# Linear attention with an ELU feature map: the program without an engine block

## The chip, the cores and the metric

The kernel runs on one core of a Trainium2 chip. A core has five engines, each with its own instruction stream: TensorE (PE, with its weight loads listed as PEld), VectorE (DVE), ScalarE (ACT), GpSimd (POOL) and SyncE (SP), which here only issues transfers. They meet through semaphores: an instruction can wait until a semaphore has a value, and can raise one when it is done. Sixteen DMA engines carry what the queues issue. The metric is the device time of one execution in microseconds (us), as the median of several runs; less is better. One execution more was recorded by the hardware profiler, and all rows quoted below come from it.

## The reference

For each of 32 heads with 2048 rows of 128 numbers, in bfloat16:

```python
phi_q = jnp.where(q > 0, q + 1, jnp.exp(q)) + 1e-6
phi_k = jnp.where(k > 0, k + 1, jnp.exp(k)) + 1e-6
kv  = einsum("bhsd,bhse->bhde", phi_k, v)      # 128 x 128 per head
z   = sum of phi_k over s                      # 128 per head
num = einsum("bhqd,bhde->bhqe", phi_q, kv)
den = einsum("bhqd,bhd->bhq", phi_q, z)[..., None] + 1e-6
return num / den
```

q, k, v and the output are 16.8 MB each, so 67 MB go through the DMA engines.

## The kernel before

A head is one step of a software pipeline. SP loads k, v and q of a head (512 KB each, line 389), ACT takes exp(k), DVE and POOL make phi(k) from it, PE accumulates phi(k)ᵀ·[1|v] into PSUM (line 428) and transposes q (line 452), ACT and DVE make phi(q) from the transposed q, PE multiplies it with the head's kv (lines 499 and 500), DVE divides (lines 522 to 540), and SP stores 512 KB (line 587). Six buffers hold inputs, ten hold outputs, so that several heads are in flight.

The order is written out by hand. Each operation is added to a `Plan` with an engine and a number, its key; `order` sorts the operations of each engine by key, and `emit` works out which semaphore values each operation has to wait for and writes the five streams. `run(e, eng)` in `emit` writes one stream: for each operation its waits (line 220), then the operation. The stream of PE has a loop in its middle: `run_loop` (line 197) emits the operations of six heads once and lets PE go over them five times, with registers that hold the semaphore values to wait for (lines 190 and 203). The other streams are written out in full. At the end of SP's stream stand waits for all output transfers (line 226), one for each of the eleven semaphores of the stores.

Where the streams stand in the program is what this change is about. The program has a main body. Building the program object (line 616) puts into it four small POOL memsets of constants and a barrier of all engines: each of the other four drains and raises one semaphore, POOL waits for four of these and raises a second semaphore by four, and each of the others waits for that. Then `nc.Block()` (line 320) opens a block; `@block.gpsimd`, `@block.sync` and so on open a body for each engine, which its engine enters by a branch out of the main body. When the block is closed, at the end of the `with` of line 284, each engine branches to a common end, where the same kind of barrier stands once more: drain, raise, and wait for the release by POOL. Instructions of that closing barrier carry line 284, those of the opening one line 616.

Of the kernel before, what the change touches and what calls it, by code (L numbers as in the profile page):

```python
# [20 lines left out]
class Plan:  # L21
# [10 lines left out]
    def add(self, eng, key, emit, reads=(), writes=(), dma=None, tag=None, kind=None, after=()):  # L32
        op = Op()
        op.eng, op.key, op.emit, op.dma, op.tag = eng, key, emit, dma, tag
        op.kind = kind or eng
        op.deps, op.needed, op.clock = list(after), False, None
        op.reads, op.writes = tuple(reads), tuple(writes)
        for r in op.reads:
            w = self.writer.get(r)
            if w is not None:  # L40
                op.deps.append(w)
            if r[0].startswith("bank"):
                op.deps += [x for x in self.readers.get(r, []) if x.eng != eng]
        for r in op.writes:
            w = self.writer.get(r)
            if w is not None and (w.eng != eng or w.dma):
                op.deps.append(w)
            op.deps += [x for x in self.readers.get(r, []) if x.eng != eng or x.dma]
        for r in op.reads:
            self.readers.setdefault(r, []).append(op)  # L50
        for r in op.writes:
            self.writer[r] = op
            self.readers[r] = []
        self.ops.append(op)
        return op
# [4 lines left out]
            out.setdefault(op.eng, []).append((op.key, i, op))  # L60
        return {e: [o for _, _, o in sorted(l, key=lambda x: x[:2])] for e, l in out.items()}

    def emit(self, nc, block, sems, dma_sem, loop):
        order = self.order()
        for op in self.ops:
            for d in op.deps:
# [65 lines left out]
        def sem_of(s):  # L132
            return dma_sem(s[1:]) if s[0] == "dma" else sems[s[0]]

        def emit_op(e, eng, op):
            last = op.emit(eng)
            if op.dma:
                last.then_inc(dma_sem(op.dma), 16)
            elif op.sem is not None:
                last.then_inc(sems[op.kind], 1)  # L140
# [25 lines left out]
        def set_up(e, eng, l0, n, turns):  # L166
            body = turns_of(order[e], l0, n, turns)
            most, step, entry, now = {}, {}, [], {}
            for _, row in body:
                for x, v, d in row:  # L170
                    assert step.setdefault(x, d) == d
                    most[x] = max(v, most.get(x, 0))
            for x, v in most.items():
                now[x] = v - step[x]
                if 0 < now[x] and order[e][l0 - 1].clock.get(x, 0) < now[x]:
                    entry.append((x, now[x]))
            asks, ends = [], {}
            for i, (_, row) in enumerate(body):
                ask = []
                for x, v, d in row:  # L180
                    if v > now[x]:
                        now[x] = v
                        ask.append((x, (d, v)))
                        ends[(d, v)] = i
                asks.append(ask)
            reg = {}
            for k, (d, v) in enumerate(ends):
                assert v > 0
                reg[(d, v)] = eng.alloc_register(f"turn_{k}")
                self.moves.append(lambda r=reg[(d, v)], v=v: eng.reg_mov(r, v))  # L190
            return body, asks, ends, entry, reg

        def run_loop(e, eng, turns, ready):
            body, asks, ends, entry, reg = ready
            for x, v in entry:
                eng.wait_ge(sem_of(x), v)
            with nc.Fori(0, turns, engines=OrderedEngineSet([eng.engine])):
                for i, (op, _) in enumerate(body):
                    for x, key in asks[i]:
                        eng.wait_ge(sem_of(x), reg[key])  # L200
                    for key, l in ends.items():
                        if l == i:
                            eng.reg_add(reg[key], reg[key], key[0])
                    emit_op(e, eng, op)

        def run(e, eng):
            ops, i = order[e], 0
            if e == "pe":
                l0, l1 = (next(x for x in range(len(ops)) if ops[x].tag == t) for t in loop[:2])
                turns = loop[2]  # L210
                assert (l1 - l0) % turns == 0
                ready = set_up(e, eng, l0, (l1 - l0) // turns, turns)
            while i < len(ops):
                if e == "pe" and i == l0:
                    run_loop(e, eng, turns, ready)
                    i = l1
                    continue
                op = ops[i]
                for s, v in waits[id(op)]:
                    eng.wait_ge(sem_of(s), v)  # L220
                emit_op(e, eng, op)
                i += 1
            if e == "sp":
                for name, n in counts.items():
                    if name[0] == "o":
                        eng.wait_ge(dma_sem(name), 16 * n)

        if "pool" in order:
            @block.gpsimd
            def _(g):  # L230
                run("pool", g)
        if "sp" in order:
            @block.sync
            def _(g):
                run("sp", g)
        if "act" in order:
            @block.scalar
            def _(g):
                run("act", g)
        if "pe" in order:  # L240
            @block.tensor
            def _(g):
                run("pe", g)
        if "dve" in order:
            @block.vector
            def _(g):
                run("dve", g)


def bass_standalone__linear_attn_elu__prompt_kernel(  # L250
# [18 lines left out]
    LAST = NH - 1  # L269
# [14 lines left out]
    with ExitStack() as es:  # L284
        def sb(name, shape, dt):
# [23 lines left out]
        sems = {e: es.enter_context(nc.semaphore(f"s_{e}")) for e in (  # L309
            "pool", "act", "pe", "dve", "emk", "rk", "phik", "kvs", "zs", "eq", "rq", "relu", "emq", "div0", "div2", "phix")}  # L310
# [6 lines left out]
            for i in range(c):  # L317
                dsems[(n, i)] = es.enter_context(nc.semaphore(f"s_{n}{i}"))

        block = es.enter_context(nc.Block())  # L320
        pl = Plan()

        def rows(x, h):
# [275 lines left out]
                store(0, 9, late, (0, 1, 2), bo)  # L599
                store(9, NT, late + 0.01, (3, 4, "t"), NBO)  # L600

        pl.emit(nc, block, sems, dma_sem, (("kv2", 1), ("num", LAST - 1), 5))


# [26 lines left out]
```

## Time and profile before

| | |
|---|---|
| time, median of 3 runs | 169.31 us (169.19 to 170.59) |
| the profiled execution's own time | 169.59 us |
| its span, from the first to the last instruction | 167.8 us |
| PE, DVE, ACT busy | 158.3, 154.2, 156.0 us |
| POOL busy | 100.8 us |
| DMA over the span | 67.25 MB, mean 401 GB/s |

The time of an execution is longer than the span, since it also holds what lies before the first and after the last instruction of the program. Busy time counts the work of the engines alone: waits, branches, drains, register moves and the issuing of transfers are not in it. Where such an instruction has a row, its engine has a q behind its name (SPq, PEldq): the row is that of the engine's sequencer. L284 is line 284 of the kernel. Starts in rows are in us from the start of the span, durations in ns where the row says so.

### The profile page before, as it was taken

The page shows a single profiled execution, that of the slowest core. Times are in us where ns is not written, and L with a number is a line of the kernel's source. Part 1 is how long each engine was busy: PE and PEld are TensorE (multiplying, and loading weights), DVE is VectorE, ACT ScalarE, POOL GpSimd, SP SyncE. Part 2 cuts the span into 40 slices and gives each one's busy share as a digit, 9 for nine tenths or more (in the row PEclk, how much of TensorE's full clock was granted, in tenths as well). Part 3 has the DMA queues.
Part 4 walks back from the last instruction along what each step waited for, and adds up shares of the span by engine and source line. Part 5 has one row for each costly group of instructions (what it writes and reads, how often), then busy time and mean ns, then how long its engine had stood idle before and what let it go on. Part 6 is the DMA issues. An engine that isn't in the chain of part 4 may idle for free.

```text
span 167.8 us, 6512 instructions
## 1 busy us (share of the span) xinstructions
PE 158.3 (94%) x3143; PEld 151.3 (90%) x2449; DVE 154.2 (92%) x302; ACT 156.0 (93%) x143; POOL 100.8 (60%) x69
## 2 busy tenths in 40 slices
PE   7579999999999999999999999999999999999960
PEld 0259999999999999999999999999999999999950
DVE  0479999999999999999999999999999999999991
ACT  3969999999999999999999999999999999998790
POOL 2405677666666776666677766666777666666300
PEclk9999999999999999999999999999999999999996
DMA  5999999999999999999999999999999999999975
GB/s 192 367 419 421 413 410 416 413 421 408 414 417 416 419 418 417 421 419 416 414 419 421 415 417 422 416 417 420 418 419 419 420 415 417 421 418 415 410 242 221
DMA packets 19885, 67.25 MB, mean 401 GB/s; under 512 B 2082, under 2 KB 2210, under 8 KB 19874
## 3 DMA queue, kind: packets, MB, share of 16 engines
q1 hardware_dynamic: 19872, 67.12, 99.4%
q8 instruction: 5, 0.08, 0.2%
q14 instruction: 6, 0.05, 0.1%
q10 hardware_dynamic: 2, 0.00, 0.0%
HBM read 50.33 MB, written 16.78 MB: 400 GB/s over the span
## 4 chain that ended last, share of the span: by engine, by line
PE 85%; DVE 5%; DMA 4%; ACT 1%; SPq 1%; issue 0%; DVEq 0%
PE kvz_ps L428 35%; PE o_ps L499 17%; PE o_ps L500 16%; PE xT_ps L452 15%; DMA k_sb<-in_k_dram 4%; DVE o_sb L540 3%; PE kvz_ps L346 1%; ACT ek_sb L396 1%; SPq L389 1%; DVE rden_sb L528 1%; DVE rq_sb L472 0%; DVE emq_sb L484 0%; DVE den_sb L522 0%; DVE emk_sb L402 0%; DVE o_sb L533 0%
## 5 line engine op out<-in xcount | busy, mean ns | idle before, releaser
L407 POOL TENSOR_TENSOR rk_sb<-rk_sb,emk_sb 128x640 bf16<-128x640 bf16 x30 | 41.9, 1397 | 45.8 <-DVE emq_sb L484 44.5
L428 PE MATMUL kvz_ps<-v_sb,rk_sb 128*128 128x128 bf16 (+1 forms) x512 | 68.0, 218 | 0.9 <-DVE rk_sb L407 0.9
L540 DVE TENSOR_TENSOR o_sb<-o_ps,rden_sb 128x768 bf16<-128x768 f32 (+2 forms) x62 | 67.8, 1134 | 0.0
L399 POOL TENSOR_SCALAR rk_sb<-k_sb 128x2048 bf16<-128x2048 bf16 x31 | 58.7, 1895 | 9.5 <-DMA k_sb<-in_k_dram 9.5
L396 ACT ACTIVATE ek_sb<-k_sb 128x2048 bf16<-128x2048 bf16 x32 | 61.5, 1921 | 3.0 <-DMA k_sb<-in_k_dram 2.9
L463 ACT ACTIVATE eq_sb<-xT_ps 128x2048 bf16<-128x2048 bf16 (+1 forms) x33 | 60.1, 1825 | 3.3 <-PE xT_ps L452 2.2
L500 PE MATMUL o_ps<-kvs_sb,rq_sb 128*128 128x129 bf16 (+1 forms) x536 | 61.1, 217 | 0.0
L499 PE MATMUL o_ps<-kvs_sb,emq_sb 128*128 128x129 bf16 (+1 forms) x536 | 61.1, 217 | 0.0
L346 PE MATMUL kvz_ps<-ones_sb,rk_sb 128*128 128x1 bf16 x428 | 58.5, 165 | 0.0
L428 PE MATMUL kvz_ps<-v_sb,emk_sb 128*128 128x128 bf16 (+1 forms) x334 | 53.9, 218 | 0.8 <-DVE emk_sb L402 0.7
L499 PEld LDWEIGHTS o_ps<-kvs_sb,emq_sb 128*128 128x128 bf16 x536 | 50.6, 98 | 0.0
L500 PEld LDWEIGHTS o_ps<-kvs_sb,rq_sb 128*128 128x128 bf16 x536 | 50.1, 97 | 0.0
L428 PEld LDWEIGHTS kvz_ps<-v_sb,rk_sb 128*128 128x128 bf16 x512 | 46.4, 96 | 3.0 <-DVE rk_sb L407 1.8
L346 PE MATMUL kvz_ps<-ones_sb,emk_sb 128*128 128x1 bf16 x253 | 41.5, 165 | 0.0
L452 PE MATMUL xT_ps<-ident,q_sb 128*128 128x128 bf16 x512 | 33.8, 219 | 1.2 <-DMA q_sb<-in_q_dram 0.9
L452 PEld LDWEIGHTS xT_ps<-ident,q_sb 128*128 128x128 bf16 x512 | 29.9, 98 | 5.4 <-DMA q_sb<-in_q_dram 4.4
L428 PEld LDWEIGHTS kvz_ps<-v_sb,emk_sb 128*128 128x128 bf16 x334 | 32.1, 96 | 1.1 <-DVE emk_sb L402 0.8
L470 ACT ACTIVATE rq_sb<-xT_ps 128x1024 bf16<-128x1024 bf16 x30 | 30.5, 1018 | 0.0
L402 DVE TENSOR_SCALAR emk_sb<-ek_sb 128x2048 bf16<-128x2048 bf16 x32 | 21.9, 683 | 5.2 <-ACT ek_sb L396 5.2
L472 DVE TENSOR_SCALAR rq_sb<-xT_ps 128x1024 bf16<-128x1024 bf16 x34 | 23.3, 690 | 0.6 <-ACT eq_sb L463 0.6
L484 DVE TENSOR_SCALAR emq_sb<-eq_sb 128x2048 bf16<-128x2048 bf16 x32 | 22.0, 688 | 0.0
L533 DVE TENSOR_TENSOR o_sb<-o_ps,rden_sb 128x128 bf16<-128x128 f32 x31 | 9.0, 291 | 1.1
(29 smaller groups left out, 52.2 us busy)
## 6 DMA issues: line engine op xcount, KB each, us to landing
k_sb<-in_k_dram SPq DMA_DIRECT2D x32, 512.0 KB, 14.4
q_sb<-in_q_dram SPq DMA_DIRECT2D x32, 512.0 KB, 14.1
v_sb<-in_v_dram SPq DMA_DIRECT2D x32, 512.0 KB, 14.4
out_dram<-o_sb SPq DMA_DIRECT2D x30, 512.0 KB, 15.1
out_dram<-o_sb SPq DMA_DIRECT2D x1, 288.0 KB, 3.2
out_dram<-o_sb SPq DMA_DIRECT2D x1, 256.0 KB
out_dram<-o_sb SPq DMA_DIRECT2D x1, 224.0 KB, 3.1
out_dram<-o_sb SPq DMA_DIRECT2D x1, 204.0 KB
```

What stands on the lines that cost most here:

```text
L346: return pe.add_instruction(mybir.InstMatmult(start_tensor_calc=start, stop_tensor_calc=stop, ldweights=False, bass_skip_group_check=True, ...
L396: lambda a, bi=bi, b2=b2: a.activation(ek_sb[:, b2, :], k_sb[:, bi, :], ACT.Exp),
L399: lambda e, bi=bi, b3=b3: e.tensor_scalar(rk_sb[:, b3, :], k_sb[:, bi, :], BIG, 0.0, op0=ALU.min, op1=ALU.max),
L407: pl.add(eng, key, lambda e: e.tensor_tensor(out=rk_sb[:, b3, c], in0=rk_sb[:, b3, c], in1=emk_sb[:, b3, c], op=ALU.add), reads=[("emk", b ...
L428: last = pe.matmul(kvz_ps[:, 1 - l:NC + r], lhsT=w, rhs=v_sb[:, bi, c - l:c + D + r], start=first, stop=fin, skip_group_check=True)
L452: last = pe.transpose(xT_ps[:, j * P:(j + 1) * P], q_sb[:, bi, j * P:(j + 1) * P], ident[:])
L463: halves[part] = pl.add("act", key, lambda a: a.activation(eq_sb[:, b2, c], xT_ps[:, c], ACT.Exp), reads=both[part:part + 1] or both, writ ...
L470: f = lambda a: a.activation(rq_sb[:, b3, c], xT_ps[:, c], ACT.Relu)
L472: f = lambda d: d.tensor_scalar(rq_sb[:, b3, c], xT_ps[:, c], 0.0, None, op0=ALU.max)
L499: pe.matmul(o_ap, lhsT=emq_sb[:, b3, t * P:(t + 1) * P], rhs=kvs_sb[:, b3, c0:c1], start=True, stop=False)
L500: return pe.matmul(o_ap, lhsT=rq_sb[:, b3, t * P:(t + 1) * P], rhs=kvs_sb[:, b3, c0:c1], start=False, stop=True)
L540: pl.add("dve", key, lambda d: d.tensor_tensor(out=o_sb[:, bo, 3 * g0:3 * g1, :].rearrange("p (a b) d -> p a b d", b=3), in0=_ap(full, bas ...
```

## The change

The block is gone. `emit` is no longer handed a block, and writes the five streams one after the other into the main body, right behind the opening barrier; PE comes last, since its loop opens new parts of the program, and whatever is written behind them would stand there too. The operations, their order on each engine, their waits and PE's loop are as before. Behind the last instruction of an engine nothing follows: no branch to a common end, no drain, and no barrier.

```diff
-    def emit(self, nc, block, sems, dma_sem, loop):
+    def emit(self, nc, sems, dma_sem, loop):
...
-        if "pool" in order:
-            @block.gpsimd
-            def _(g):
-                run("pool", g)
-        if "sp" in order:
-            @block.sync
-            def _(g):
-                run("sp", g)
-        if "act" in order:
-            @block.scalar
-            def _(g):
-                run("act", g)
-        if "pe" in order:
-            @block.tensor
-            def _(g):
-                run("pe", g)
-        if "dve" in order:
-            @block.vector
-            def _(g):
-                run("dve", g)
+        for e, eng in (("pool", nc.gpsimd), ("sp", nc.sync), ("act", nc.scalar), ("dve", nc.vector), ("pe", nc.tensor)):
+            run(e, eng)
...
-        block = es.enter_context(nc.Block())
...
-        pl.emit(nc, block, sems, dma_sem, (("kv2", 1), ("num", LAST - 1), 5))
+        pl.emit(nc, sems, dma_sem, (("kv2", 1), ("num", LAST - 1), 5))
```

## The prediction

> **What bounds the kernel now.** The time of three stages has to be told apart: the start, the long middle, and the end. The first view is the table by windows, with cuts at the first transfer (0.8 us), at the full pipeline (13 us), at the last heads (156 us), at the last compute (164.2 us) and at the last wait for a transfer (167.4 us). Columns are the window, its length, the busy time of PE, PEld, DVE, ACT and POOL with the number of instructions, PE's clock, the DMA share and GB/s.
>
> ```profile
> 0.00:0.80 0.80, 0.00 (x0) 0.00 (x0) 0.00 (x0) 0.00 (x0) 0.27 (x5) 1.00 0.00 0
> 0.80:13.00 12.20, 9.24 (x91) 3.86 (x59) 5.91 (x13) 8.43 (x7) 2.77 (x5) 1.00 0.92 350
> 13.00:156.00 143.00, 142.88 (x2938) 141.66 (x2296) 140.35 (x271) 140.28 (x119) 96.95 (x60) 1.00 1.03 417
> 156.00:164.20 8.20, 6.19 (x123) 5.82 (x97) 7.89 (x21) 7.28 (x18) 0.81 (x1) 1.00 0.87 324
> 164.20:167.40 3.20, 0.00 (x0) 0.00 (x0) 0.00 (x0) 0.00 (x0) 0.00 (x0) 0.56 0.54 209
> 167.40:167.80 0.40, 0.00 (x0) 0.00 (x0) 0.00 (x0) 0.00 (x0) 0.00 (x0) 0.50 0.00 0
> ```
>
> In the middle, PE is busy for 142.88 of 143.00 us, and the DMA engines are full too. The change touches no operation there, so those 143 us move only if PE is held up by its own instruction stream; that is the third rival below. What the change does touch lies in the first window, in which the opening barrier ends and the streams are entered, and in the last one, 0.40 us in which no engine computes and no transfer runs. Behind the span there is more: the execution took 169.59 us, the span 167.8, so 1.79 us lie before the first or after the last instruction, and no row shows how they are shared out.
>
> The second view is the chain of work that ended last, with the page's head.
>
> ```profile
> span 167.8 us, 6512 instructions
> ...
> PE 85%; DVE 5%; DMA 4%; ACT 1%; SPq 1%; issue 0%; DVEq 0%
> ```
>
> The 85% for PE is the middle. This chain is followed back from the last computing instruction, so the end barrier is not in it and has to be read from the rows of its line, and from the waits of SP's queue.
>
> **The end, row by row.** The instructions of the closing barrier carry line 284. Columns: engine, instruction, count, duration in ns (min/median/max), first and last start in us.
>
> ```profile
> L284 POOLq EVENT_SEMAPHORE  x2: 17/17/17, 167.6 to 167.7; - x2
> L284 POOLq DRAIN  x1: 1502/1502/1502, 155.4 to 155.4; - x1
> L284 PEldq DRAIN  x1: 723/723/723, 161.7 to 161.7; - x1
> L284 ACTq DRAIN  x1: 911/911/911, 163.1 to 163.1; - x1
> L284 DVEq DRAIN  x1: 1091/1091/1091, 163.1 to 163.1; - x1
> L284 SPq COMPARE_BRANCH  x1: 38/38/38, 167.4 to 167.4; - x1
> L284 SPq DRAIN  x1: 7/7/7, 167.6 to 167.6; - x1
> L284 SPq EVENT_SEMAPHORE  x1: 17/17/17, 167.7 to 167.7; - x1
> L284 ACTq EVENT_SEMAPHORE  x1: 17/17/17, 167.7 to 167.7; - x1
> L284 DVEq EVENT_SEMAPHORE  x1: 21/21/21, 167.7 to 167.7; - x1
> L284 PEldq EVENT_SEMAPHORE  x1: 51/51/51, 167.7 to 167.7; - x1
> ```
>
> The waits for the stores, and what SP waited for there:
>
> ```profile
> L226 SPq EVENT_SEMAPHORE  x5: 28/28/28, 164.6 to 167.3; - x5
> ```
>
> ```profile
> SPq L226 <- DMA out_dram<-o_sb: 2.5, 1, 2.5
> ...
> SPq L284 <- PEq L284: 0.2, 1, 0.2
> ```
>
> The reader is to see who comes last. Four engines drained long before: POOL's drain starts at 155.4, PE's at 161.7, ACT's and DVE's at 163.1 us, and each has ended by 164.2 (163.1 plus 1.09). SP waits 2.5 us for the stores and passes the last wait of line 226 at 167.3. Then comes the hand-over: SP's branch at 167.4, its drain at 167.6, POOL's two semaphore instructions at 167.6 and 167.7, and the four releases at 167.7, of which PE's is the longest with 51 ns and closes the span at 167.8. Nothing covers this: the window from 167.4 on is empty.
>
> **What the change removes there.** Line 226 has only five semaphore rows. A branch waits for nothing of its own kind, and it stands where the wait for the eleventh store semaphore has to be; I take it that this last wait rides on the branch. Without a branch it needs an instruction of its own, priced by its neighbours at 28 ns against the branch's 38. So what remains is a wait at 167.4, and the span ends at its end. Removed are the 0.40 us of the last window less the branch's own 0.04: **0.36 us**. The starts are rounded to 0.1 us, so by the rows alone the term lies between 0.26 and 0.46. What is late next is the same store: its landing sets the time of SP's last wait, and nothing in the change moves a store.
>
> The four drains that go too cost nothing, as they lie beside the stores' 3.20 us; the cover would be gone only if an engine drained after 167.4. DVE's drain of 1091 ns starts ahead of its last division's end and waits for it, not the other way about, so the last store starts no earlier without it.
>
> **The start.** The opening barrier (line 616) stays, and SP's first load comes straight behind it.
>
> ```profile
> L616 POOLq EVENT_SEMAPHORE  x2: 17/17/17, 0.5 to 0.6; - x2
> ...
> L616 SPq EVENT_SEMAPHORE  x1: 17/17/17, 0.7 to 0.7; - x1
> L616 ACTq EVENT_SEMAPHORE  x1: 17/17/17, 0.7 to 0.7; - x1
> L616 DVEq EVENT_SEMAPHORE  x1: 21/21/21, 0.7 to 0.7; - x1
> L616 PEldq EVENT_SEMAPHORE  x1: 51/51/51, 0.7 to 0.7; - x1
> ```
>
> ```profile
> 0.73 0.39 SPq L389 DMA_DIRECT2D k_sb<-in_k_dram  x1
> 1.18 0.42 SPq L389 DMA_DIRECT2D q_sb<-in_q_dram  x1
> ```
>
> Had the branches into the block been executed, there would be a branch row for each engine here; neither line 616 nor line 284 has one at the start. The release is at 0.7 and the first load at 0.73, while the second load comes 0.06 us after the first ended (1.12 to 1.18), so the gap ahead of the first is no longer than the plain distance of two of SP's instructions. I price the entry at 0. The ends are 0 and, if SP did lose something between 0.65 and 0.73, a gain of 0.08. The opening barrier also gives the closing one a second price: from POOL's first semaphore instruction (0.5) to the last release (0.7 and 51 ns) it took 0.2 to 0.3 us, to which SP's branch and drain come at the end. That agrees with 0.36.
>
> **The sum.** Against the profiled execution: 169.59 − 0.36 − 0 = 169.23 us. That execution lies 0.28 above the median of the three runs, so the time to expect is 169.31 − 0.36 = **168.95 us**, 0.2% less. The three runs of before spread over 1.4 us, so about 1% is what a measurement of this kernel can tell from no change, and the forecast is "within 1%".
>
> **The rivals.**
>
> *More goes than the span shows.* After the change four engines reach their end between 157 and 164 us, and only SP at 167.4. If each engine has closing work behind its last instruction, that of four engines moves beside the stores, and out of the 1.79 us outside the span a part goes as well. For it: that stretch exists and today all engines enter it together. Against: SP has the same work and is still last; only engines slower at it than SP can give a gain. Half of it, 0.9 us, gives 169.31 − 0.36 − 0.9 = 168.05; all of it, 167.16.
>
> *The barrier is paid under another name.* Something behind the program still has to know that all engines are done. If that costs SP's signal and a release as now, the span is shorter by 0.36 and the stretch behind it longer by as much: 169.31. For it: 1.79 us outside the span are more than nothing. Against: whatever stands there stood there before too, behind the kernel's own barrier, so the two were paid one after the other. The Trainium skill, Runtime: NRT & Kernel Launch, section The ~15µs preamble/postamble breakdown, says that the runtime closes each launch with a barrier of its own over all engines, at about 1.5 us. By that rule the wait for all engines stays whatever the kernel does, and whether this rival or the forecast holds depends on whether the four early engines can stand in that barrier already; no row of this trace shows it.
>
> *PE's loop has to fetch its code again (slower).* PE's stream is moved from the block's body into the main body; its loop head may come to lie elsewhere in what the engine holds of its code. The rows of code fetches, from the view of DMA queues for 0 to 45 us and then for 45 to 168 us, and of the loop's closing branch:
>
> ```profile
> q8 instruction: 5, 0.08, 0.7%
> q14 instruction: 1, 0.01, 0.0%
> ```
>
> ```profile
> q14 instruction: 5, 0.04, 0.1%
> ```
>
> ```profile
> L197 PEldq COMPARE_BRANCH  x5: 76/213/231, 41.9 to 156.9; - x5
> ```
>
> Queue q8 fetched five pieces of 16 KB by 45 us and none after, so I take it for PE's, and the loop was held whole: four times PE jumped back (the fifth branch, the one of 76 ns, falls through), and the middle's 0.12 us of idle time show no stall. One fetch takes 0.7% of 16 engines for 45 us, 5.0 us, over five pieces: 1.0 us. If the moved loop no longer fitted, each of four returns would wait for at least one piece, and PE has no slack in the middle: 4 × 1.0 − 0.36 = 3.6 us more, 172.95. It decides as soon as the jump's target is no longer held; a single stall at the loop's entry would give 168.95 + 1.0 = 169.95. Against it: if the entry branches left no instruction behind, PE's stream ahead of the loop is as long as before. The same page of the Trainium skill, section Instruction fetch mechanics, says that a taken branch whose target isn't in a window of two pages forces a fetch before execution goes on. By that rule the four jumps, over some 28.75 us of work each, would have paid already; the trace disagrees, with 0 pieces of q8 behind 45 us.
>
> **How the numbers follow.** The forecast gets 0.60 (168.6 to 169.2), the larger gain 0.20 (167.2 to 168.6), no gain 0.12 (169.2 to 169.6), and the loop 0.08, of which 0.05 for the returns and 0.03 for one stall at the entry. Faster by over 1% means below 167.6, the far part of the larger gain: 0.05. Slower by over 1%, above 171.0: the returns, 0.05. The rest is 0.90. The range runs from 168.1, which takes in half of the larger gain, to 169.6, the end of no gain: 0.60 + 0.12 + 0.10 = 0.82.
>
> **What would show it.** Right: no row of line 284, the span at about 167.4, its last instruction a wait of line 226 (now six such rows) at 167.4 and 28 ns; the first load still at 0.73; five pieces on q8, all by 45 us; the middle at PE's 142.9 us of 143. The first rival shows as a distance between time and span well below 1.79, the second as one of 2.15. The third shows as pieces on q8 after 45 us and idle PE behind the branches, at 41.9 us and every 28.75 us from there ((156.9 − 41.9) / 4). I am wrong if any of the middle's period changes, or if engines that end early do something that reaches the stores: then the last wait's 167.4 moves.

## The result and the profile after

The changed kernel takes 168.38 us (168.18 to 168.99, 8 runs) against 169.39 us (169.13 to 170.59, 8 runs) before: ratio 0.9935, 95% interval 0.9908 to 0.9962. Run again on another occasion, it took 168.54 against 169.32 us, ratio 0.9956 (0.9940 to 0.9973). So it is faster by 0.8 to 1.0 us, about half a per cent and clear of the noise, where 0.36 was forecast.

Each run gives its time and its span, so the gain can be parted in two. Before, in 29 runs taken beside the rerun, the median span was 167.5 us and the time outside the span, that is time less span, 1.81 us on average (1.75 to 1.87). After, over the 14 runs of both occasions, the median span is 167.15 and the time outside 1.31 us (1.26 to 1.37). The span fell by 0.35, the time outside by 0.50, together 0.85 us. The time outside differs by about 0.1 us from run to run, so its fall is clear in every single run; the fall of the span has to be read from medians, since spans of one kernel differ by more than that.

The windows of the profiled execution after (168.30 us, span 167.0), from the full pipeline on, cut at the last heads, the last compute and the last wait; the columns are as before the change:

```profile
13.00:156.00 143.00, 142.89 (x2931) 141.45 (x2294) 140.30 (x270) 139.69 (x119) 96.93 (x60) 1.00 1.03 417
156.00:163.90 7.90, 5.93 (x118) 5.58 (x92) 7.64 (x20) 7.26 (x18) 0.56 (x1) 1.00 0.87 335
163.90:166.97 3.07, 0.00 (x0) 0.00 (x0) 0.00 (x1) 0.00 (x0) 0.00 (x0) 0.65 0.56 215
166.97:167.00 0.03, 0.00 (x0) 0.00 (x0) 0.00 (x0) 0.00 (x0) 0.00 (x0) 0.50 0.00 0
```

The middle is as full as before, PE busy 142.89 of 143.00 us. The last window, 0.40 us before, is 0.03 us long: one wait. The rows of a closing barrier are gone, and the waits for the stores have six rows (eleven semaphores, so some rows hold more than one), the last of them at the span's end:

```profile
L226 SPq EVENT_SEMAPHORE  x6: 17/28/1880, 164.3 to 167.0; - x6
```

At the start nothing has moved. The opening barrier (now line 597) releases SP at 0.7 us as before, and SP's first load after the change is this one:

```profile
0.73 0.39 SPq L370 DMA_DIRECT2D k_sb<-in_k_dram  x1
...
```

The two profiled spans differ by 0.8 us, more than the medians do. The last window explains 0.37 of it. The other 0.43 lies ahead of the last window: the last store was issued 0.3 us earlier (163.9 against 164.2), and it landed 3.0 us after its issue, against 3.1. PE was ahead by 0.3 us already at its loop's first branch (41.6 against 41.9 us), and this came in at the start, where ACT waits for k of the second head. The rows of the exp(k) that starts then, from the timelines of before, of the changed kernel, and of the changed kernel run again:

```profile
9.35 1.91 ACT L396 ACTIVATE ek_sb<-k_sb 128x2048 bf16<-128x2048 bf16 x1 [1.23 <-DMA k_sb<-in_k_dram]
```

```profile
8.84 1.91 ACT L377 ACTIVATE ek_sb<-k_sb 128x2048 bf16<-128x2048 bf16 x1 [0.82 <-DMA k_sb<-in_k_dram]
```

```profile
8.10 1.91 ACT L377 ACTIVATE ek_sb<-k_sb 128x2048 bf16<-128x2048 bf16 x1
```

The same program started it at 8.84 once and at 8.10 another time, and the kernel before with a second barrier at its end (below) at 8.34. But an earlier start did not bring an earlier end. The changed kernel run again issued its last store at 163.2, 0.7 us earlier than the first time, and its span is 167.2, longer than 167.0, because this store took longer to land. Its rows from the first and the second profile of the changed kernel (KB, us from issue to landing):

```profile
out_dram<-o_sb SPq DMA_DIRECT2D x1, 224.0 KB, 3.0
```

```profile
out_dram<-o_sb SPq DMA_DIRECT2D x1, 224.0 KB, 3.9
```

So when the first loads and the last store land differs from one execution to the next, and a single pair of profiles can't price a change of 0.4 us.

### The profile page after: what moved, and what is told of

The parts are those of the page before. It is cut to its first block, busy times and chain, and to the rows that moved or that the text cites. A ratio compares the mean times of both kernels' runs of the same rounds, so it can differ in the third digit from the quotient of the medians.

```text
span 167.0 us, 6501 instructions
## 1 busy us (share of the span) xinstructions
PE 158.5 (95%) x3143; PEld 151.4 (91%) x2449; DVE 154.3 (92%) x302; ACT 155.9 (93%) x143; POOL 100.8 (60%) x69
## 4 chain that ended last, share of the span: by engine, by line
PE 86%; DVE 6%; DMA 4%; ACT 1%; SPq 1%; issue 0%; DVEq 0%
PE kvz_ps L409 36%; PE o_ps L480 17%; PE o_ps L481 17%; PE xT_ps L433 16%; DMA k_sb<-in_k_dram 4%; DVE o_sb L521 3%; PE kvz_ps L327 1%; ACT ek_sb L377 1%; SPq L370 1%; DVE rden_sb L509 1%; DVE o_sb L514 0%; DVE rq_sb L453 0%; DVE emq_sb L465 0%; DVE den_sb L503 0%; DVE emk_sb L383 0%
## 5 line engine op out<-in xcount | busy, mean ns | idle before, releaser
L388 POOL TENSOR_TENSOR rk_sb<-rk_sb,emk_sb 128x640 bf16<-128x640 bf16 x30 | 41.9, 1396 | 46.1 <-DVE emq_sb L465 44.8
```

What stands on the lines that cost most here:

```text
L388: pl.add(eng, key, lambda e: e.tensor_tensor(out=rk_sb[:, b3, c], in0=rk_sb[:, b3, c], in1=emk_sb[:, b3, c], op=ALU.add), reads=[("emk", b ...
```

## The experiments

Two theories stood against each other. **The end:** all of the gain comes from four engines ending early; the closing barrier held them, and each has something to do behind its last instruction that counts into the time. **The place of the code:** the part outside the span comes from the streams standing in the main body. A third, that a barrier as such costs 1 us, goes by the same runs.

**The barrier put back, without the block.** Added to the changed kernel:

```diff
         pl.emit(nc, sems, dma_sem, (("kv2", 1), ("num", LAST - 1), 5))
+        nc.all_engine_barrier()
```

> The changed kernel with one barrier of all engines behind its last wait, and still no block. Theory 'the end': the whole gain comes from four engines ending early, 0.36 to 0.43 us inside the span and 0.5 us behind it. Then the time is that of the kernel before within 0.2 us: span up by 0.35 to 0.4, outside back at 1.8 us. Rival 'the place of the code': the gain outside the span comes from the streams standing in the main body without branches into a block. Then outside stays at 1.3 us, and the time is 0.5 us below the kernel before.

Measured: 169.19 us against 169.32 before, ratio 0.9994 (0.9976 to 1.0012), and 1.80 us outside the span in its 11 runs. The place of the code falls: the streams stand in the main body, and the whole 0.50 outside the span is back. The rows of its barrier (line 584), and of its waits for the stores:

```profile
L584 POOLq EVENT_SEMAPHORE  x2: 17/17/17, 167.6 to 167.7; - x2
L584 POOLq DRAIN  x1: 1502/1502/1502, 155.3 to 155.3; - x1
...
L584 SPq DRAIN  x1: 7/7/7, 167.6 to 167.6; - x1
...
```

```profile
L226 SPq EVENT_SEMAPHORE  x6: 17/28/1991, 164.5 to 167.5; - x6
```

The expectation missed one size. The median span, 167.4, is 0.15 above the changed kernel's on the same chip (167.25), not 0.35 to 0.4; against all 14 runs of the changed kernel (167.15) it is 0.25. Medians of so few runs can't decide between these, since the spans of this version alone lie between 167.2 and 168.4. The rows are sharper: from the last wait at 167.5 to the span's end at 167.8 lie about 0.3 us, and SP's drain comes right behind the wait. In the kernel before, SP's branch stood between, at 167.4 with the drain only at 167.6. So by these rows, whose starts are rounded to 0.1 us, some 0.1 of the forecast's 0.36 was the way out of the block, and the rest the barrier. The times can't tell that 0.1 from nothing (0.9976 to 1.0012).

**A second barrier in the kernel before.** Added behind the closed block:

```diff
         pl.emit(nc, block, sems, dma_sem, (("kv2", 1), ("num", LAST - 1), 5))
+    nc.all_engine_barrier()
```

> The kernel before with a second barrier of all engines behind the block's. Theory 'the end': the span grows by the barrier's own hand-over alone, 0.2 to 0.3 us (from POOL's first semaphore instruction to the last release), and the time outside stays at 1.8 us, since all engines ended late already: 0.2 to 0.3 us slower than before (ratio 1.0015). Rival 'each barrier costs 1 us': the time grows by as much as the change took off, 1.0 us (ratio 1.006).

Measured: 169.59 against 169.32, ratio 1.0020 (1.0008 to 1.0032); median span 167.8 against 167.5; 1.80 us outside. A barrier in which nobody is early costs 0.27 us (by the interval, 0.14 to 0.54), its hand-over. Its rows (line 603), behind those of the block's:

```profile
L603 POOLq EVENT_SEMAPHORE  x2: 17/17/17, 167.6 to 167.7; - x2
L603 POOLq DRAIN  x1: 46/46/46, 167.5 to 167.5; - x1
L603 SPq DRAIN  x1: 7/7/7, 167.5 to 167.5; - x1
...
L603 PEldq EVENT_SEMAPHORE  x1: 51/51/51, 167.8 to 167.8; - x1
```

From the drains at 167.5 to the last release at 167.8: 0.3 us, in line with the difference of the times. That a barrier costs 1 us each time falls with it.

**All engines late, without a barrier.** In the changed kernel each engine, not SP alone, waits for the stores at its end:

```diff
-            if e == "sp":
+            if True:
                 for name, n in counts.items():
                     if name[0] == "o":
                         eng.wait_ge(dma_sem(name), 16 * n)
```

> The changed kernel in which all five engines, not SP alone, wait for the eleven store semaphores at their end; no barrier. Theory 'the end': the span is that of the changed kernel within 0.1 us (no hand-over), but all engines now end late, so the time outside goes back to 1.8 us: 0.5 us slower than the changed kernel. Rival 'the barrier itself': only drains and the hand-over cost, so the time outside stays at 1.3 us and the time is that of the changed kernel.

Beside it, on the same chip, ran the changed kernel again:

> The changed kernel once more, beside the experiments. Both theories: 1.0 us less than the kernel before (ratio 0.994), span near 167.0 us, and 1.3 us outside the span (1.8 in the kernel before).

Measured: 168.91 us (12 runs) with all engines waiting, 168.54 (6 runs) with SP alone. The median span is 167.05 against 167.25, so no cost shows inside; outside it is 1.83 against 1.31 us. The rows of line 226 show all five leaving the last wait together:

```profile
L226 POOLq EVENT_SEMAPHORE  x6: 17/42/1962, 159.5 to 166.9; - x6
L226 PEldq EVENT_SEMAPHORE  x6: 51/51/1962, 160.7 to 166.9; - x6
L226 ACTq EVENT_SEMAPHORE  x6: 17/38/1962, 162.1 to 166.9; - x6
L226 DVEq EVENT_SEMAPHORE  x6: 21/50/1964, 162.1 to 166.9; - x6
L226 SPq EVENT_SEMAPHORE  x6: 17/28/1962, 163.6 to 166.9; - x6
```

So the 0.50 us is neither drain nor hand-over: it is the price of engines other than SP ending late, with a barrier or without one. The span and the time outside are two terms, and this run moves the second.

**Which engine.** The eleven waits were moved from SP to one other engine each, by the same line (`if e == "pe":` and so on), and then given to all but POOL (`if e != "pool":`).

> The changed kernel with the eleven last waits on PE in place of SP, so that PE alone ends late. Theory 'one slow engine': each engine has closing work of its own length behind its last instruction, and the 1.8 us of the kernels in which all end late is that of the slowest, SP's being 1.3. If PE is the slowest: 1.8 us outside, time 0.5 us above the changed kernel; if not, 1.3 or less. Rival 'a chain': the closing is a hand-over from engine to engine, and what it costs depends on where in the chain the late engine stands; then the five engines give five values in steps, between some 0.9 and 1.8.

> The changed kernel with the eleven last waits on ACT in place of SP. Theory 'one slow engine': 1.3 us outside the span or less, unless ACT is the slow one (1.8). Rival 'a chain': a value of its own, a step away from those of the other engines.

> The changed kernel with the eleven last waits on DVE in place of SP. Theory 'one slow engine': 1.3 us outside the span or less, unless DVE is the slow one (1.8). Rival 'a chain': a value of its own, a step away from those of the other engines.

> The changed kernel with the eleven last waits on POOL in place of SP. Theory 'one slow engine': 1.3 us outside the span or less, unless POOL is the slow one (1.8). Rival 'a chain': a value of its own, a step away from those of the other engines. On any of the four: if it stays below SP's 1.3 us, the version is faster than the changed kernel by the difference.

> The changed kernel in which PE, ACT, DVE and SP wait for the stores at their end, and POOL alone ends early. Theory 'the slowest late engine sets it': with POOL out, the next slowest of those that were late alone sets the time outside the span, PE with 1.58 us; the span is the changed kernel's. Rival 'the number of late engines counts': four late engines cost more than PE alone, near the 1.8 us of all five.

Time outside the span, mean of all runs of each (lowest to highest). The rows come from three chips: SP's and the last two from one, the four other single engines from a second, all but POOL from a third. The kernel before, run beside them, had 1.81, 1.79 and 1.82 us there, so the chips differ by some 0.03:

| engines that end late | outside, us | runs | ratio to the kernel before |
|---|---|---|---|
| SP (the changed kernel, again) | 1.31 (1.26 to 1.37) | 6 | 0.9956 (0.9940 to 0.9973) |
| DVE | 1.41 (1.37 to 1.45) | 10 | 0.9960 (0.9931 to 0.9989) |
| ACT | 1.43 (1.40 to 1.47) | 6 | 0.9963 (0.9930 to 0.9996) |
| PE | 1.58 (1.52 to 1.64) | 10 | 0.9970 (0.9944 to 0.9997) |
| POOL | 1.85 (1.80 to 1.89) | 10 | 0.9971 (0.9949 to 0.9994) |
| all but POOL | 1.57 (1.52 to 1.60) | 10 | 0.9973 (0.9948 to 0.9998) |
| all five, by waits | 1.83 (1.78 to 1.90) | 12 | 0.9984 (0.9964 to 1.0004) |
| all five, by a barrier in the main body | 1.80 (1.76 to 1.86) | 11 | 0.9994 (0.9976 to 1.0012) |

POOL is the slow one: alone it costs as much as all five together, and without it the four cost as much as PE alone. So the slowest engine that ends late sets the time outside, and their number does not count. The expectation that the others would all lie at 1.3 or below was wrong: the price depends on the engine, though DVE and ACT lie too close to be told apart. The rival of a chain foresaw five values but from 0.9 up; none is below SP's 1.31, and the distances (0.10, 0.02, 0.15, 0.27) are no even steps. Whether a price is the length of an engine's own closing work or its place in some hand-over behind the program isn't told apart by these runs. The ratios are too wide to rank the versions, since they hold the scatter of the spans; the column of the time outside ranks that term alone, and by it the changed kernel, with SP last, is the best of them.

## Why the prediction was right, and where it fell short

*The forecast's size.* The prediction gave its largest chance, 0.60, to 168.6 to 169.2 us. The measured 168.38 and 168.54 lie in the band of the first rival, to which it gave 0.20. That the wider range held is owed to the room left for this rival, not to the sum.

*The middle: right, the end not bound by it alone.* PE's middle is full before and after, 142.88 and 142.89 of 143 us. But of the two profiles of the changed kernel, the one that computed 0.7 us ahead ended 0.2 later, as its last store landed later; a time of compute can't simply be added up to the end.

*The last wait at 167.4.* The prediction named a move of it as a sign of being wrong, and in the profile it moved to 166.97. But the last wait of the kept profiles scatters: it starts at 166.9 with all engines waiting and at 168.3 with PE or DVE alone. The median spans, 167.5 and 167.15, differ by what the removed hand-over explains, so no run shows that the change reached the stores.

*The removed hand-over, 0.36 us: right.* The last window went from 0.40 to 0.03 us, the median span from 167.5 to 167.15. That the eleventh wait rode on SP's branch agrees too: line 226 now has the sixth row that was missing. What the step had not parted is the block's exit, by the rows some 0.1, from the barrier, some 0.27.

*The drains cost nothing: right.* They lay beside the stores, and POOL's still starts at 155.3 with the barrier back.

*The entry at 0: right, for a weaker reason than given.* The first load starts at 0.73 as before; with the streams in the main body and the barrier back, time and time outside are those of before. The missing branch rows could not have shown it: at the closing of the block, line 284 has a branch row for SP alone, so the way out of the other four engines left no row either.

*The time outside the span taken as fixed: wrong, and the term that is missing from the sum.* The forecast carried the 1.79 us over unchanged; they fell to 1.31. This was the first rival, at 0.20. That part of the time outside goes when engines end early is what the runs showed; its size was put at 0.9 and measured 0.50. The argument set against it, that SP has the same work and only engines slower at it can give a gain, held and should have been turned round: nothing spoke for SP being the slowest of five. With the term, put in afterwards, the sum is 169.31 − 0.36 − 0.50 = 168.45, beside 168.38 and 168.54 measured.

*The barrier under another name: wrong here.* The time outside fell and did not grow by 0.36. The Trainium skill, Runtime: NRT & Kernel Launch, section The ~15µs preamble/postamble breakdown, has a barrier of all engines behind every launched program. If that barrier is what the time outside holds, the early engines get through their share of it while SP waits for the stores. No row shows that stretch, so this reading stays an argument.

*The loop fetching its code again: did not happen.* The code fetches after the change, for 0 to 45 us and then 45 to 167 us, and the loop's branch:

```profile
q8 instruction: 5, 0.08, 0.7%
...
```

```profile
q14 instruction: 5, 0.04, 0.1%
```

```profile
L197 PEldq COMPARE_BRANCH  x5: 76/213/227, 41.6 to 156.7; - x5
```

On q8, which the prediction took for PE's, five pieces by 45 us and none after, the same branch times but for the longest (227 against 231 ns), and (156.7 − 41.6) / 4 = 28.78 us for a turn against 28.75. The other queue, q14, fetched as many pieces as before too.

## What to carry to other kernels

Look at what stands between the last transfer's landing and the end of the time, in the span and outside it: here 0.36 us of hand-over, and 0.50 us that depended on which engines ended late, were paid for no work. Let only the engine that is cheapest to end last wait for the last store (here SP), and let the others, POOL above all, run out of instructions earlier. When the difference between time and span changes, treat it as a term of its own: it scatters by some 0.1 us where the span of one kernel scatters by 0.8 (after) to 1.6 (before).

## What the runs showed of the hardware

The time behind or around the span isn't a constant of the chip: it depended on which engine ended last, from 1.31 us (SP) over 1.41 (DVE), 1.43 (ACT) and 1.58 (PE) to 1.85 (POOL), the slowest late engine deciding. What an engine does in that time, no row shows. A barrier of all engines in which nobody was early took 0.27 us. Over the eleven profiles, whose first load starts at 0.73 us in each, the start of the second head's exp(k) moved between 7.96 and 9.44 us, and the last store of 224 KB took between 3.0 and 4.2 us to land; each scatters by more than the whole change, and the earlier start did not go with the earlier end.
